# Linear attention, gated feed-forward and soft mixture on one core: where two kinds of early work stand in the VectorE and ScalarE queues

## The chip, the cores and the metric

One core of a Trainium2 chip. The metric is the device time of one execution in microseconds; the kernel as it was takes 327.0 us (median of 3 runs, 326.41 to 327.06).

## What is computed

Three layers on 4352 tokens (4 batches of 1088) of 128 features; every weight and activation is float32 at the interface.

```python
# attention with a feature map phi(x) = outer(S1 x, S2 x), 64 features per head
kv = einsum('bhsf,bhsd->bhfd', phi(k), v);  z = phi(k).sum(s)
x  = (phi(q) @ kv) / (phi(q) . z + 1e-6)
# gated feed-forward, d_ff = 1536
xn = x / sqrt(mean(x*x) + 1e-6) * rms_g
y  = (silu(xn @ w_gate) * (xn @ w_val)) @ w_out
# soft mixture of 8 experts with 4 slots each: softmax over tokens, expert MLP, softmax over slots
out = combine(y @ phi, experts(dispatch(y @ phi).T @ y))
```

S1, S2 and the three feed-forward weights arrive as 64-bit floats and are put together on the chip from their 32-bit words.

## The kernel before: tiles, stages and the order of the work

**Tiles and slots.** The tokens form nine tiles: tiles 0 to 7 hold 512 tokens each (two to a batch), tile 8 holds the 256 tokens left over. Within a tile the feed-forward goes over the 12 blocks of 128 of d_ff. One (tile, block) pair is a slot; slots are counted from 0 here, so slot 9 is the tenth and slots 0 to 11 are tile 0. In the main loop (`for i in range(n_slots + LAG)`) a slot does, on TensorE, a gate and a value product of three matmuls each (`mm3`, L621 to L623: high part by high part, high by low, low by high); on ScalarE the silu (L651); on VectorE the product of silu and value (L652, `ff_gate`), which reads the value's PSUM bank, of which there are two; and two slots later the product with w_out (`ff_out`). For tile 0, `ff_out` uses the whole w_out in two passes (L676, tile `ring`); only from tile 1, slot 12, does it use the split w_out, `woh` and `wol` (L621 to L623 with output `o`).

**Weights.** `w_keys` lists nine groups: gv0, o0, gv1, gv2, o1, gv3, gv4, o2, gv5. A gv group is 256 columns of w_gate and w_val and feeds two slots (gv1 slots 2 and 3, gv5 slots 10 and 11); an o group is a third of w_out. `f64_words` converts a group: two ScalarE passes (L189, L192), three VectorE passes (L194, L196, L198), an add on GpSimd (L202, in two pieces). `split_w` then makes the high part on ScalarE (L238, a cast) and the low part on GpSimd (L244, two pieces; for gv0 on VectorE, L246). For w_out, `split_o` calls `split_w` for the three groups in a row; it is put on the list of conversion steps at slot 9 (`if i == NF - 3`), so its three casts and six subtractions are written in the program after slot 9's `ff_gate`.

**Keys and queries.** `k_chain(b)` works for batch b (1 to 3; batch 0 is done ahead): two half groups g of VectorE transposes (`k.transpose`, L336, two instructions each, into tile `T`), a projection on TensorE (L354), feature products on VectorE (L282), sums on TensorE (L384), and at last the table `kvz` (L421). The odd 64 tokens of a batch go through TensorE (L339), a copy on ScalarE (L342, also into `T`) and L354. Batch 1's chain is spawned at slot 0 with a start at slot 8, so its transposes are written after the `ff_gate` of slot 9 (g = 0) and of slot 11 (g = 1); batch 2's after slots 25 and 27, batch 3's after slots 49 and 51. `q_chain(T)` prepares tile T's x: a transpose of the queries (`shuffle`, L492, also into `T`), a projection (L497), products, L520 against `kvz`, division, root (L566, L567 on GpSimd), scaling (L571), a TensorE transpose (L576), and the high and low parts xh (L581) and xl (L582). Tile `T` has two buffers for all of these.

**What sets the order.** After the first slot the code fixes no order of its own: a planner places each engine's instructions by its own estimate of when they are ready, and among ready ones takes the one written first. Each engine then runs its queue strictly in that order. `tc.issue_after(x)` puts what is traced inside it, as far as it runs on x's engine, behind x in that queue; it adds no wait for x to finish. `mark` holds such x: `mark["silu"]` the latest silu (ScalarE), `mark["gate", T, f]` the product of a slot (VectorE).

Of the kernel before, what the change touches and what calls it, by code (L numbers as in the profile page):

```python
# [12 lines left out]
ALU = mybir.AluOpType  # L13
# [35 lines left out]
def body(ctx, tc, q, k, v, s1, s2, wg, wv, wo, rg, phi, w1, w2, out):  # L49
    nc = tc.nc  # L50
    pe, act, dve, pool = nc.tensor, nc.scalar, nc.vector, nc.gpsimd
# [17 lines left out]
    def row(tag, bufs=1, dt=F32):  # L69
        return sb.tile([P, 512], dt, tag=tag, name=tag, bufs=bufs)  # L70
# [3 lines left out]
    gate = [None]  # L74
# [102 lines left out]
    mark = {}  # L177
# [38 lines left out]
    def conv_w(key):  # L216
        kind, i = key
        if kind == "gv":
            w = row("cvt", 2)
        else:  # L220
            if i % 2 == 0:
                wo_full[0] = ring()
            w = wo_full[0][:, 512 * (i % 2) : 512 * (i % 2) + 512]
            wo32.append(w)
        s, r = row("cvs", 2).bitcast(U32), row("cvc", 2).bitcast(U32)
        yield from f64_words(stage.pop(key), w, s, r, w.bitcast(U32))
        if kind == "gv":
            yield from split_w(key, w, dve if i == 0 else pool)

    def split_w(key, w, low):  # L230
        kind, i = key
        if kind == "gv":
            dh, dl = (t[:, :, 256 * i : 256 * (i + 1)] for t in (wgh, wgl))
            src = w.rearrange("p (m n) -> p m n", m=2)
        else:
            dh, dl = (t[:, 4 * i : 4 * i + 4, :] for t in (woh, wol))
            src = w.rearrange("p (c n) -> p c n", c=4)
        act.copy(dh, src)  # L238
        yield
        if low is pool:  # L240
            k = PIECE // src.shape[2]
            for t in range(0, src.shape[1], k):
                ts = slice(t, t + k)
                pool.tensor_tensor(out=dl[:, ts], in0=src[:, ts], in1=dh[:, ts].bitcast(F32), op=ALU.subtract)  # L244
        else:
            low.tensor_tensor(out=dl, in0=src, in1=dh.bitcast(F32), op=ALU.subtract)  # L246
        yield

    def split_o():

        for i, w in enumerate(wo32):
            yield from split_w(("o", i), w, pool)
# [188 lines left out]
    def k_chain(b):  # L441
        k = Keys(b)
        with tc.issue_after(mark["word"]):
            k.zero()
            for hp in range(2):
                k.copy_v(hp, pool.tensor_copy)
        for g in range(2):
            if g == 1:
                k.transpose(2)
            yield POST, 1  # L450
            k.transpose(g)
            if g == 1:
                k.copy(2)
            yield PE, 0
            k.project(g)
            yield POST, 1
            k.halves(g)
            k.outer(g)
            yield PE, 0
        k.project(2)  # L460
        yield POST, 1
        k.halves(2)
        k.outer(2)
        yield PE, 0
        for hp in range(2):
            k.sum(hp, range(9))
            yield PE, 1
        yield POST, 0
        k.spread()
        yield PE, 0  # L470
        k.back()
        yield POST, 1
        k.place()
        kv_done.add(b)
# [142 lines left out]
    hh, hl, hf32 = {}, {}, {}  # L617
# [15 lines left out]
    def pieces(T, f):  # L633

        return [slice(0, 256), slice(256, 512)] if (T, f) == (8, NF // 2 - 1) else [slice(0, 512)]
# [11 lines left out]
    def ff_gate(T, f):  # L647
        s = row("silu", 2)
        hf32[T, f] = row("hh", 3, F32R).bitcast(F32) if T == 0 and f < WHOLE else row("hf", 2)
        for g, v, cs in zip(gps.pop((T, f)), vps.pop((T, f)), pieces(T, f)):  # L650
            mark["silu"] = act.activation(s[:, cs], g[:, cs], AF.Silu).ins  # L651
            mark["gate", T, f] = dve.tensor_tensor(out=hf32[T, f][:, cs], in0=v[:, cs], in1=s[:, cs], op=ALU.mult).ins  # L652

    def whole(T, f):

# [246 lines left out]
    def start_tile(T):  # L902
# [9 lines left out]
        if T % 2 == 0 and T // 2 + 1 < B:  # L912
            b = T // 2 + 1
            load_k(b)
            load_q(b)
            load_kr(b)
            load_v(b)
            spawn(k_chain(b), PE, 8 if b == 1 else 0)
# [28 lines left out]
    for i in range(n_slots + LAG):  # L947
        now = base + i
        if i < n_slots:
            T, f = slots[i]  # L950
# [10 lines left out]
        if i < n_slots:  # L961
            in_order(ff_gate, T, f)
# [179 lines left out]
    for T in range(NTILE):  # L1142
# [10 lines left out]
        o = [ps.tile([P, 512], F32, tag="gv"[(T + e) % 2], name="fo", bufs=2) for e in range(2 if T == 0 else 1)]  # L1153
# [14 lines left out]
        if T < 8:  # L1168
            b, hf = T // 2, T % 2
            nc.sync.dma_start(  # L1170
                out=out[S * b : S * b + 1024].rearrange("(p j) d -> p j d", j=8)[:, 4 * hf : 4 * hf + 4, :], in_=ob
            )
        else:
            for hf in range(2):
                nc.sync.dma_start(
                    out=out.rearrange("(u e s) d -> e s u d", u=2, e=2)[hf, 1024:], in_=ob[64 * hf : 64 * hf + 64, 0:2, :]
# [31 lines left out]
```

## Time and profile before

| what | value |
|---|---|
| runs | 326.41, 327.06, 327.0 us (median 327.0) |
| the profiled execution: its own time | 326.61 us |
| its span in the profile | 324.8 us |
| TensorE busy | 312.0 us, 96% |
| VectorE / ScalarE / GpSimd busy | 237.5 / 185.4 / 61.2 us |
| granted TensorE clock, mean | 0.986 |

The span leaves 1.8 us of the execution's own time outside. Times in rows are microseconds from the start of the span. PE is TensorE, DVE VectorE, ACT ScalarE, POOL GpSimd, SP the engine that issues the loads. L12 is line 12 of the kernel. A number in brackets at the end of a timeline row is the engine's idle time just before it and what ended it. A granted clock of 1.00 is 2.4 GHz, 0.50 is 1.2 GHz.

### The profile page before, as it was taken

Reading aid. Unit: us, or ns where it says so; the run is one execution under the profiler, and the core shown is the slowest. Engines: PE = TensorE matmul, PEld = TensorE weight load, DVE = VectorE, ACT = ScalarE, POOL = GpSimd, SP = SyncE. Lnnn points to the kernel's source line nnn. Section 1 sums busy time; section 2 is a strip of 40 time slices with the busy share of each in tenths; the row PEclk is TensorE's granted clock in tenths of the full one; section 3 lists DMA queues with packets and bytes.
Section 4 is the critical chain, followed back from the end, with each engine's and each line's share of the span. In section 5 each row is a group of like instructions: output and inputs, shape, how many; then the busy total and the mean of one; then the engine's idle time right before and its main releaser. Section 6 shows DMA issues by size and latency. Waiting matters only on the chain.

```text
span 324.8 us, 5533 instructions
## 1 busy us (share of the span) xinstructions
PE 312.0 (96%) x2028; PEld 248.1 (76%) x2028; DVE 237.5 (73%) x458; ACT 185.4 (57%) x412; POOL 61.2 (19%) x104
## 2 busy tenths in 40 slices
PE   8987989999998999999999999999999999999994
PEld 6774655778886878888888778888888878897574
DVE  4779976775878785777887868678778666664663
ACT  3757464456565455665564657565656666556553
POOL 3356699700010210001001000010020100003030
PEclk9997899999999999999999999999999999999998
DMA  8988000000007000000070000000890394000007
GB/s 201 297 289 206 0 0 1 2 0 2 0 0 199 7 2 0 2 0 0 2 198 5 3 0 2 0 0 6 279 251 3 78 339 103 0 2 0 2 3 274
DMA packets 31131, 22.40 MB, mean 69 GB/s; under 512 B 13056, under 2 KB 27136, under 8 KB 31104
## 3 DMA queue, kind: packets, MB, share of 16 engines
q1 hardware_dynamic: 31072, 22.04, 23.6%
q8 instruction: 16, 0.26, 0.3%
q14 instruction: 11, 0.09, 0.1%
q10 hardware_dynamic: 32, 0.00, 0.0%
HBM read 19.81 MB, written 2.23 MB: 68 GB/s over the span
## 4 chain that ended last, share of the span: by engine, by line
PE 75%; issue 6%; DVE 5%; DMA 1%; POOL 1%; ACT 1%; DVEq 0%; SPq 0%; POOLq 0%
PE v L621 6%; PE g L621 6%; PE v L622 6%; PE g L622 6%; PE v L623 6%; PE g L623 6%; PE o L621 6%; PE o L622 6%; PE o L623 6%; PE aux L520 3%; PE aux L384 2%; PE aux L354 2%; PE aux L497 2%; PE o L676 2%; PE fo L1159 1%
## 5 line engine op out<-in xcount | busy, mean ns | idle before, releaser
L651 ACT ACTIVATE silu<-g 128x512 f32<-128x512 f32 (+1 forms) x103 | 60.5, 592 | 41.1 <-PE g L623 38.6
L661 ACT CAST hh<-hf 128x512 fp32r<-128x512 f32 x89 | 55.0, 617 | 42.3 <-DVE hf L652 38.8
L666 DVE TENSOR_TENSOR hl<-hf,hh 128x512 fp32r<-128x512 f32 x89 | 60.9, 685 | 22.4 <-ACT hh L661 21.0
L652 DVE TENSOR_TENSOR hf<-v,silu 128x512 f32<-128x512 f32 (+1 forms) x91 | 61.8, 680 | 19.7 <-PE v L623 9.5
L621 PE MATMUL v<-xh,wgh 128*128 128x512 f32 (+1 forms) x108 | 44.0, 408 | 2.1 <-DVE hh L652 1.6
L621 PE MATMUL g<-xh,wgh 128*128 128x512 f32 (+1 forms) x108 | 42.8, 402 | 1.0 <-ACT wgh L238 1.0
L622 PE MATMUL g<-xh,wgl 128*128 128x512 f32 (+1 forms) x108 | 42.7, 395 | 0.0
L622 PE MATMUL v<-xh,wgl 128*128 128x512 f32 (+1 forms) x108 | 42.1, 390 | 0.0
L623 PE MATMUL g<-xl,wgh 128*128 128x512 f32 (+1 forms) x108 | 41.4, 384 | 0.0
L623 PE MATMUL v<-xl,wgh 128*128 128x512 f32 (+1 forms) x108 | 41.0, 381 | 0.0
L621 PE MATMUL o<-hh,woh 128*128 128x512 f32 (+1 forms) x94 | 36.8, 392 | 0.0
L623 PE MATMUL o<-hl,woh 128*128 128x512 f32 (+1 forms) x94 | 36.6, 389 | 0.0
L622 PE MATMUL o<-hh,wol 128*128 128x512 f32 (+1 forms) x94 | 35.7, 380 | 0.0
L566 POOL TENSOR_SCALAR rs<-ss 128x4 f32<-128x4 f32 (+1 forms) x9 | 2.6, 290 | 138.8 <-ACT sq L561 137.2
L621 PEld LDWEIGHTS v<-xh,wgh 128*128 128x128 f32 x108 | 20.6, 190 | 8.7 <-DVE hh L652 3.8
L621 PEld LDWEIGHTS g<-xh,wgh 128*128 128x128 f32 x108 | 20.3, 191 | 5.8 <-ACT wgh L238 1.9
L622 PEld LDWEIGHTS g<-xh,wgl 128*128 128x128 f32 x108 | 20.6, 191 | 4.7 <-issue 0.8
L622 PEld LDWEIGHTS v<-xh,wgl 128*128 128x128 f32 x108 | 20.3, 188 | 4.7 <-issue 1.3
L623 PEld LDWEIGHTS g<-xl,wgh 128*128 128x128 f32 x108 | 20.6, 191 | 4.3 <-issue 0.5
L623 PEld LDWEIGHTS v<-xl,wgh 128*128 128x128 f32 x108 | 20.3, 188 | 4.6 <-issue 0.7
L621 PEld LDWEIGHTS o<-hh,woh 128*128 128x128 f32 x94 | 17.7, 188 | 3.0
L623 PEld LDWEIGHTS o<-hl,woh 128*128 128x128 f32 x94 | 17.7, 188 | 3.0
(254 smaller groups left out, 522.2 us busy)
## 6 DMA issues: line engine op xcount, KB each, us to landing
ring<-in_moe_w_dram SPq DMA_DIRECT2D x12, 256.0 KB, 6.5
ring<-in_moe_w_dram SPq DMA_DIRECT2D x5, 512.0 KB, 5.4
ring<-in_k_dram SPq DMA_DIRECT2D x8, 256.0 KB, 3.0
qt<-in_q_dram SPq DMA_DIRECT2D x4, 512.0 KB, 5.3
ring<-in_v_dram SPq DMA_DIRECT2D x16, 128.0 KB, 4.7
ring<-in_moe_w_gate_dram SPq DMA_DIRECT2D x6, 256.0 KB, 6.3
ring<-in_moe_w_val_dram SPq DMA_DIRECT2D x6, 256.0 KB, 6.5
ring<-in_moe_w_out_dram SPq DMA_DIRECT2D x3, 512.0 KB, 6.2
```

The lines of the kernel that those rows point to most:

```text
L354: pe.matmul(o, self.kT[g][:, P * t : P * t + pp], bdf, start=True, stop=True)
L384: pe.matmul(self.a["kv", hp][64 * h2 : 64 * h2 + D1, 64 * hp : 64 * hp + 64], va[:, h, 2 * i + g, :] if t < 8 else vr[:, h, :], self.pk[hp ...
L497: pe.matmul(self.a["q"][:, 64 * h : 64 * h + 64], self.qD[:, P * h : P * h + P], bdf, start=True, stop=True)
L520: pe.matmul(o, pD[:, f, h, :], rhs, start=(f == 0), stop=(f == 1))
L621: first = pe.matmul(o, ah, bh, start=start, stop=False)
L622: pe.matmul(o, al, bh, start=False, stop=False)
L623: last = pe.matmul(o, ah, bl, start=False, stop=stop)
L651: mark["silu"] = act.activation(s[:, cs], g[:, cs], AF.Silu).ins
L652: mark["gate", T, f] = dve.tensor_tensor(out=hf32[T, f][:, cs], in0=v[:, cs], in1=s[:, cs], op=ALU.mult).ins
L661: act.copy(hh[T, f], hf32[T, f])
L666: dve.tensor_tensor(out=hl[T, f], in0=hf32.pop((T, f)), in1=hh[T, f].bitcast(F32), op=ALU.subtract)
L676: last = pe.matmul(ops[T][:, 0:w], w_c, h[:, cs], start=(c == 0), stop=(c == NF - 1))
```

## The change

Three places, all of them order alone; no operand, size, engine or transfer is touched. The casts of w_out's split are queued behind the silu of the slot at which they are written (slot 9). Each pair of VectorE key transposes (g = 0 and 1, all three later batches) is queued behind the last product of silu and value written before it. `mark["gate"]` is new and holds that product.

```diff
@@ split_w
-        act.copy(dh, src)
+        with tc.issue_after(mark["silu"]) if kind == "o" else nullcontext():
+            act.copy(dh, src)
@@ k_chain
             yield POST, 1
-            k.transpose(g)
+            with tc.issue_after(mark["gate"]):
+                k.transpose(g)
@@ ff_gate
-            mark["gate", T, f] = dve.tensor_tensor(out=hf32[T, f][:, cs], in0=v[:, cs], in1=s[:, cs], op=ALU.mult).ins
+            mark["gate"] = mark["gate", T, f] = dve.tensor_tensor(out=hf32[T, f][:, cs], in0=v[:, cs], in1=s[:, cs], op=ALU.mult).ins
```

## Rows read from the trace of the kernel before

**Rows 1.** Page, part 1: busy us, share of the span and instructions

```profile
PE 312.0 (96%) x2028; PEld 248.1 (76%) x2028; DVE 237.5 (73%) x458; ACT 185.4 (57%) x412; POOL 61.2 (19%) x104
```

**Rows 2.** Stretches: length, busy us of each engine, PEclk, DMA share, GB/s

```profile
29.00:35.00 6.00, 5.47 (x10) 3.26 (x11) 5.97 (x12) 1.96 (x5) 2.26 (x4) 0.50 0.45 90
...
47.00:62.00 15.00, 14.35 (x63) 9.85 (x62) 9.13 (x11) 6.67 (x18) 14.27 (x24) 1.00 0.01 2
...
98.00:102.00 4.00, 3.13 (x17) 2.39 (x16) 2.76 (x5) 1.56 (x3) 0.00 (x0) 1.00 0.64 189
102.00:296.00 194.00, 194.00 (x1175) 160.64 (x1174) 145.54 (x268) 116.66 (x251) 12.63 (x20) 1.00 0.21 58
```

**Rows 3.** Waits of PE, whole span: waited for, total us, times, longest

```profile
PE v L621 <- DVE hh L652: 1.6, 3, 0.8
...
PE g L621 <- ACT wgh L238: 1.0, 2, 0.7
...
PE aux L354 <- DVE T L336: 0.9, 1, 0.9
...
PE aux L354 <- ACT T L342: 0.3, 1, 0.3
```

**Rows 4.** Timeline of PE, tile 0: start, us, instruction, [idle before <-releaser]

```profile
30.75 0.80 PE L621 MATMUL v<-xh,wgh 128*128 128x512 f32 x1 [0.52 <-DVE hh L652]
...
46.15 0.50 PE L621 MATMUL v<-xh,wgh 128*128 128x512 f32 x1 [0.77 <-DVE hh L652]
...
48.28 0.39 PE L621 MATMUL v<-xh,wgh 128*128 128x512 f32 x1
...
61.28 0.50 PE L622 MATMUL g<-xh,wgl 128*128 128x512 f32 x1
```

**Rows 5.** Timeline of DVE, tile 0

```profile
28.19 1.11 DVE L336 STREAM_TRANSPOSE T<-ring 128x256 f32<-128x256 f32 x2 [0.48 <-DMA ring<-in_k_dram]
29.15 0.82 DVE L194 TENSOR_SCALAR ring<-ring 128x512 f32<-128x512 f32 x1
30.00 0.69 DVE L652 TENSOR_TENSOR hh<-v,silu 128x512 f32<-128x512 f32 x1
...
31.47 0.41 DVE L194 TENSOR_SCALAR ring<-ring 128x512 f32<-128x512 f32 x1
...
32.40 1.08 DVE L336 STREAM_TRANSPOSE T<-ring 128x256 f32<-128x256 f32 x2
...
45.42 1.27 DVE L652 TENSOR_TENSOR hh<-v,silu 128x512 f32<-128x512 f32 x2
```

**Rows 6.** Timeline of POOL: w_out's low parts, and gv5's

```profile
28.26 1.42 POOL L244 TENSOR_TENSOR wol<-ring,woh 128x256 fp32r<-128x256 f32 x2
...
40.13 2.06 POOL L244 TENSOR_TENSOR wol<-ring,woh 128x256 fp32r<-128x256 f32 x2
...
56.44 1.86 POOL L244 TENSOR_TENSOR wol<-ring,woh 128x256 fp32r<-128x256 f32 x2
...
59.65 1.43 POOL L244 TENSOR_TENSOR wgl<-cvt,wgh 128x256 fp32r<-128x256 f32 x2
```

**Rows 7.** Timeline of ACT: the first of w_out's three casts

```profile
26.00 0.61 ACT L238 CAST woh<-ring 128x512 fp32r<-128x512 f32 x1
```

**Rows 8.** Timeline of DVE where tile 2 begins

```profile
100.66 1.09 DVE L336 STREAM_TRANSPOSE T<-ring 128x256 f32<-128x256 f32 x2 [1.20 <-DMA ring<-in_k_dram]
```

**Rows 9.** Timelines of PE, DVE and ACT: users of T, and of kvz

```profile
27.23 1.10 PE L497 MATMUL aux<-bd,T 128*128 128x64 f32 x8 [0.86 <-DVE T L492]
...
66.14 1.29 DVE L492 STREAM_TRANSPOSE T<-qt 128x512 f32<-128x512 f32 x2
...
94.71 1.00 PE L497 MATMUL aux<-bd,T 128*128 128x64 f32 x8
...
131.55 1.54 ACT L421 COPY kvz<-aux 32x264 f32<-32x264 f32 x4 [0.89 <-PE aux L412]
...
140.47 0.72 PE L520 MATMUL aux<-kvz,work 128*128 128x132 f32 x5
```

## The prediction

> **What bounds the kernel now.** I first read the page's busy shares: TensorE is busy 96% of the span [rows 1], so nothing but TensorE's own idle time, or time at the lower clock, can be won. Next the stretches: from 102 to 296 us it is busy without a gap [rows 2], so most of the kernel offers nothing. What is left lies in tile 0 (about 29 to 62 us) and where tile 2 begins (98 to 102 us, 0.87 us missing) [rows 2]. Then TensorE's list of waits: of the entries, those on work that the change touches or that stands near it are value matmuls waiting for VectorE's product of silu and value (1.6 us in 3 waits), gate matmuls waiting for ScalarE's cast of w_gate (1.0 us in 2), a key projection waiting for its transposes (0.9) and one waiting for the copy of the odd keys (0.3) [rows 3]. In the timeline of tile 0 the first group's waits are 0.52 us at 30.75 and 0.77 at 46.15 [rows 4]; the third is the remainder, about 0.3. So the question is what VectorE is doing when TensorE wants that product.
>
> In its queue, from 29 to 35 us VectorE is busy 5.97 of 6 us [rows 2]: there it, and not TensorE, sets the pace. And it holds key transposes of the second batch that the program writes only after slot 9's product: two at 28.19 (1.11 us, after 0.48 us of standing still for the key load) and two at 32.40 (1.08) [rows 5]. The first pair stands directly in front of what slot 0's product at 30.00 needs, and TensorE's value matmul at 30.75 waits for just that product [rows 4, 5]. On GpSimd w_out's low parts of groups o0 and o1 stand at 28.26 and 40.13, 1.42 and 2.06 us in the row of conversions [rows 6], though split weights of w_out are first read by slot 12, and slot 10 is still at its matmuls at 61.28 [rows 4].
>
> **Part 1, the transposes of batch 1.** Removed from VectorE's saturated stretch: 1.11 + 0.48 + 1.08 = 2.67 us [rows 5]. They go behind the products of slots 9 and 11, where VectorE is busy 9.13 of 15 us [rows 2], so their 2.2 us there I cost at nothing for VectorE; if that cover is gone, it costs at most these 2.2 us. Queued behind a pair there: the next product and tile 1's scaling; who waits are the batch's projections on TensorE.
>
> One thing comes in their place. Both T buffers are now free once tile 1's projection at 27.23 is done [rows 9]. Tile 3's query shuffle has no such tie, and in the trace it was taken as soon as a buffer was free: two shuffles stand at 66.14, but the projection of the second is at 94.71 [rows 9]. I expect it to move up into the early stretch, at 1.29 / 2 = 0.65 us. VectorE's net lead is then 2.67 - 0.65 = 2.0 us.
>
> **Part 2, w_out's split.** Three casts leave ScalarE's early queue. The first, at 26.00, is 0.61 us [rows 7] and stands directly before slot 0's silu; this costs nothing now, since VectorE is later still (30.00). Six subtractions leave GpSimd's row: 1.42 us ahead of gv1's low part and 2.06 us ahead of gv3's add [rows 6]. With VectorE's lead of 2.0 us, gv3's cast comes about 2 us earlier, against a wait for it of 0.3 us: 1.0 less the longest, 0.7 [rows 3], which is for gv1's cast, before anything that is moved but w_out's first cast, and which I leave. The third subtraction (1.86 us at 56.44) stands before gv5's low part at 59.65 [rows 6]. All six now come behind slot 9's silu, in 53 to 65 us. GpSimd is busy 14.27 of 15 us there [rows 2], but the only thing TensorE needs of it at once is gv5's low part; w_out's own is due at slot 12.
>
> *A rule against the rows.* VectorE's L194 took 0.82 us at 29.15, while GpSimd was at the first w_out piece, and 0.41 at 31.47 [rows 5, 6]. The Trainium skill, SBUF — State Buffer, section "Who interferes with whom", says that such a VectorE operation and a GpSimd one that reads SBUF exclude each other for a whole instruction through a shared port pair, and that one with a single SBUF input outside the fast modes doesn't. By this rule each w_out piece moved away would give VectorE up to 0.4 us besides, a lead near 3 us and no wait left in tile 0, and the sum below would be 0.2 us larger; but the next conversion moves up and collides in its stead, so I take the sum without it.
>
> **Part 3, batches 2 and 3.** Batch 2's first pair stood still 1.20 us for its load, at the head of VectorE's queue [rows 8], and TensorE's key projection then waited 0.9 us for it [rows 3]. Behind slot 25's product the load has landed, so this wait goes: between 0 and 0.87, I take 0.87. Batch 3's pair shows no wait of TensorE: nothing. No transfer is moved, and SP's queue stays; a load that is given its buffer later is not in sight, since loads wait for a tile's start.
>
> **The sum.** TensorE's idle time that goes: 0.52 at 30.75, which counts half since TensorE runs at half clock from 29 to 35 us (granted 0.50 [rows 2]) and I let that stretch stay where it is: 0.26. Then 0.77, 0.3 (cast), 0.3 (third product) and 0.87: together 2.5. Each matmul after a wait also takes 0.11 us longer (0.50 at 46.15 against 0.39 at 48.28 [rows 4]); for four, 0.45. That is 2.95 us. What comes new: batch 1's first projection now follows its transposes closely, and where a projection does, TensorE waited 0.86 (27.23 [rows 9]) or 0.9 [rows 3]; between 0 and 0.9 for each of two, in all I take 0.5. And the product at 46.15 comes later than it would need, since 0.5 + 0.3 of waits ahead of it go too and TensorE asks earlier: 0.8 + 0.8 against a lead of 2.0, close enough that I take 0.2 of a wait as left. So 2.95 - 0.5 - 0.2 = 2.25 us, say 2.3. The profiled execution took 326.61 us (span 324.8); it becomes 324.3. It was 0.4 us under the median of 327.0, so my forecast for the median is **324.7**, its own range 323.4 to 326.0.
>
> **Rivals.**
>
> *The conversions, not the transposes, hold tile 0 (smaller gain).* For it: gate casts wait for GpSimd's adds, and GpSimd is nearly full from 47 to 62 us [rows 2]. Against: the wait that I can read at 30.75 ends with VectorE. Then only batch 2's 0.87, the 0.26 and some 0.1 are won: 327.0 - 1.2 = 325.8.
>
> *w_out's pieces get in front of gv5's low part (no gain).* They now become ready at about the same time as gv5's cast. The third piece is before it already [rows 6]; the first two add 1.42 + 2.06 = 3.5 us, against a lead of 2 to 2.6, so that part ends near 62. TensorE meanwhile arrives about 2 us earlier than 61.28 [rows 4] and has no key projection left to fill the wait, so it idles near 3 us: the gain of tile 0 is gone and the 0.87 with it, 326.9. If the clock then falls as it did at 29 us, after such waits as the 0.86 at 27.23 [rows 9], half of 6 us comes on top [rows 2]: 330. The Trainium skill, TensorE: Matmul & The Clock Gate, section "HAM oscillation — how this bites in real kernels", has this rule, that waits of TensorE throttle its clock; by it the dearer of the two prices would be the right one whenever the wait is long. Against the rival: gv5's split is written earlier in the program and is taken first among ready work.
>
> *Slower: the two T buffers.* Batch 2's pairs now wait for slots 25 and 27, while tile 4's and tile 5's query shuffles are tied to nothing. If both take a T buffer before batch 2's second pair, that pair waits until a projection frees one, and a buffer was held so for 94.71 - 66.14 = 28.6 us [rows 9]. The batch's kvz is placed at 131.55 to 133.09 and first read at 140.47 [rows 9], a slack of 7.4 us. TensorE would then stall at tile 4 for anything from 0 to 21 us; I take 8: 327.0 - 2.3 + 8 = 332.7. It decides from the point where the pair comes more than 7.4 us later than now. Against it: the pair is written earlier than either shuffle, and both shuffles need the queries' load, which is issued behind the keys'.
>
> *The clock does not fall at 29 us.* Half of the 6 us at 0.50 [rows 2] is then won too, 3 us: near 322. Against: what TensorE does before 29 us is not touched.
>
> That the change doesn't do what it says I give no chance: the casts at 26.00 and the transposes at 28.19 and 32.40 stand in front of the instructions they are now tied behind.
>
> **How the numbers follow.** Forecast 0.58; conversions hold 0.16; no gain 0.10; the same with a lost clock 0.06; T buffers 0.06; clock stays 0.04. A measurement of this kernel tells about 0.2% (0.65 us) from no change, so faster means under 326.35. Faster: 0.58 + 0.16 + 0.04 = 0.78; same 0.10; slower 0.12. The range runs from 323.2 (the forecast's low end and a little) to 327.2, which takes in the case of no gain; outside stay the lost clock, the T buffers and the clock that stays, 0.16.
>
> **What would show it.** In the changed profile: no L336 on VectorE between 10 and 50 us; no w_out cast before slot 9's silu; slot 0's product done by about 29 us; TensorE's list with less than 0.6 us for value matmuls waiting for that product, no wait for a cast in tile 0 after 30 us, and no wait for batch 2's transposes at 100 us; gv5's low part before 60 us; the half-clock stretch still there and about 6 us long. I am wrong if TensorE idles at gv5's low part, if tile 0's waits only change their names, or if a gap opens at the start of tile 4.

## The result: 1% faster, a little more than forecast, and not where the forecast had put it

| | before | after |
|---|---|---|
| median of 4 runs | 326.84 us | 323.65 us |
| all runs | 326.41 to 327.06 | 323.34 to 324.17 |
| the profiled execution, its span | 326.61, 324.8 | 324.17, 322.3 |
| granted TensorE clock, mean | 0.986 | 0.991 |

The ratio is 0.9903, 95% interval 0.9887 to 0.9919: 3.2 us by the medians. The profiled executions are 2.44 us apart. Part of that difference lies ahead of everything that the change touches: the first matmul of the main loop (L621 before, L623 after, on xh) begins at 23.35 us in the trace of before and at 23.78 in that of after, and between 23.39 and 23.87 in the ten kernels below. Counted from that matmul, the copy of tile 3's output out of PSUM comes at 143.73 before and 140.72 after, 3.0 us earlier, and that is about what is left at the end. So I give the times inside tile 0 from that matmul on. Line numbers after the first place of the change have moved by one or two: L654 is the product of silu and value (before: L652), L337 a key transpose (L336), L245 a low part on GpSimd (L244), L355 the key projection (L354).

**Stretches after the change**, against [rows 2]. Columns as there: length, busy us of PE, PEld, DVE, ACT, POOL, granted clock, DMA share, GB/s.

```profile
29.00:35.00 6.00, 5.12 (x13) 3.27 (x13) 5.97 (x11) 3.00 (x7) 3.05 (x4) 0.72 0.56 124
...
47.00:62.00 15.00, 15.00 (x62) 10.41 (x61) 11.07 (x16) 7.11 (x16) 14.55 (x26) 1.00 0.01 2
...
98.00:102.00 4.00, 3.68 (x18) 2.97 (x18) 4.00 (x8) 2.52 (x6) 0.00 (x0) 1.00 1.11 287
102.00:293.00 191.00, 190.49 (x1158) 157.75 (x1158) 143.03 (x263) 114.69 (x247) 12.83 (x20) 1.00 0.20 55
```

VectorE is still without a pause from 29 to 35 us: what was taken out of its queue there was filled by the conversions behind it. The granted clock in that stretch is 0.72 where it was 0.50. From 47 to 62 us TensorE no longer pauses. From 62 to 293 us nothing was won: TensorE idles 0.32 us in 98 to 102 and 0.51 in the stretch behind, together 0.83, against 0.87 and none before [rows 2], and 0.27 us at 97.82 for a silu, where before it did not wait.

**TensorE's waits after**, against [rows 3]: waited for, total us, times, longest.

```profile
PE o L678 <- DVE hh L654: 1.1, 1, 1.1
...
PE aux L340 <- DMA kr<-in_k_dram: 0.8, 1, 0.8
...
PE v L623 <- DVE hh L654: 0.4, 1, 0.4
```

**Timeline of PE after**, against [rows 4].

```profile
29.88 2.05 PE L678 MATMUL o<-hh,ring 128*128 128x512 f32 x2 [1.11 <-DVE hh L654]
...
43.91 0.51 PE L623 MATMUL v<-xh,wgh 128*128 128x512 f32 x1 [0.41 <-DVE hh L654]
...
57.02 0.50 PE L624 MATMUL g<-xh,wgl 128*128 128x512 f32 x1
...
102.51 0.24 PE L340 MATMUL aux<-ident,kr 64*128 64x64 f32 x1 [0.83 <-DMA kr<-in_k_dram]
```

The waits for casts of w_gate are gone. The waits for the product of silu and value are not: 1.6 us in three became 0.4 in one, but the tile's w_out product, which stands first in line now, waits 1.11 us for slot 0's product at 29.88. And where tile 2 begins, the wait for batch 2's transposes [rows 3] has an heir of nearly the same length, the transpose of the odd keys on TensorE (L340), which waits 0.83 us for their load.

**Timeline of DVE after**, against [rows 5, 8]:

```profile
28.06 0.94 DVE L194 TENSOR_SCALAR ring<-ring 128x512 f32<-128x512 f32 x1
29.04 0.69 DVE L654 TENSOR_TENSOR hh<-v,silu 128x512 f32<-128x512 f32 x1
...
52.82 1.09 DVE L337 STREAM_TRANSPOSE T<-ring 128x256 f32<-128x256 f32 x2
...
59.97 1.11 DVE L337 STREAM_TRANSPOSE T<-ring 128x256 f32<-128x256 f32 x2
...
99.00 1.11 DVE L337 STREAM_TRANSPOSE T<-ring 128x256 f32<-128x256 f32 x2
```

**Timelines of POOL and ACT after**, against [rows 6, 7]:

```profile
29.45 1.62 POOL L245 TENSOR_TENSOR wgl<-cvt,wgh 128x256 fp32r<-128x256 f32 x2 [0.73 <-ACT wgh L239]
...
54.88 1.43 POOL L245 TENSOR_TENSOR wgl<-cvt,wgh 128x256 fp32r<-128x256 f32 x2
56.25 4.26 POOL L245 TENSOR_TENSOR wol<-ring,woh 128x256 fp32r<-128x256 f32 x6
...
51.57 1.65 ACT L239 CAST woh<-ring 128x512 fp32r<-128x512 f32 x3
```

The order is the one that the change asks for. Batch 1's transposes stand behind products of tile 0, without any wait of their own, and the projections that follow them on TensorE, at 55.88 and 64.09, show no wait either. The six pieces of w_out's low part come in one row at 56.25, directly behind gv5's low part at 54.88: gv5's part ends at 56.3, and TensorE asks for it at 57.02. That is a margin of 0.7 us, of which more below.

### The profile page after: what moved, and what is told of

The parts are those of the page before. It is cut to its first block, busy times and chain, and to the rows that moved or that the text cites. A ratio compares the mean times of both kernels' runs of the same rounds, so it can differ in the third digit from the quotient of the medians.

```text
span 322.3 us, 5538 instructions
## 1 busy us (share of the span) xinstructions
PE 310.7 (96%) x2028; PEld 247.8 (77%) x2028; DVE 237.0 (74%) x458; ACT 185.0 (57%) x412; POOL 61.3 (19%) x104
## 4 chain that ended last, share of the span: by engine, by line
PE 78%; issue 5%; DVE 2%; DMA 1%; SPq 1%; POOL 0%; ACT 0%; DVEq 0%; POOLq 0%
PE v L623 7%; PE g L624 6%; PE v L624 6%; PE g L625 6%; PE v L625 6%; PE g L623 6%; PE o L623 6%; PE o L625 6%; PE o L624 6%; PE aux L522 4%; PE o L678 3%; PE aux L385 2%; PE aux L355 2%; PE aux L499 2%; DMA kr<-in_k_dram 1%
## 5 line engine op out<-in xcount | busy, mean ns | idle before, releaser
L654 DVE TENSOR_TENSOR hf<-v,silu 128x512 f32<-128x512 f32 (+1 forms) x91 | 61.3, 679 | 20.4 <-PE v L625 11.4
L623 PE MATMUL v<-xh,wgh 128*128 128x512 f32 (+1 forms) x108 | 44.1, 408 | 0.8 <-DVE hh L654 0.4
L623 PE MATMUL g<-xh,wgh 128*128 128x512 f32 (+1 forms) x108 | 43.4, 406 | 0.3 <-ACT silu L653 0.3
L624 PE MATMUL g<-xh,wgl 128*128 128x512 f32 (+1 forms) x108 | 42.0, 389 | 0.0
L623 PE MATMUL o<-hh,woh 128*128 128x512 f32 (+1 forms) x94 | 36.8, 392 | 0.0
L568 POOL TENSOR_SCALAR rs<-ss 128x4 f32<-128x4 f32 (+1 forms) x9 | 3.0, 333 | 132.4 <-ACT sq L563 130.8
L623 PEld LDWEIGHTS v<-xh,wgh 128*128 128x128 f32 x108 | 20.5, 190 | 6.6 <-DVE hh L654 1.2
L623 PEld LDWEIGHTS g<-xh,wgh 128*128 128x128 f32 x108 | 20.6, 191 | 5.7 <-ACT silu L653 1.0
L624 PEld LDWEIGHTS o<-hh,wol 128*128 128x128 f32 x94 | 17.7, 188 | 2.9
```

Of the source, the lines that this page charges most:

```text
L623: first = pe.matmul(o, ah, bh, start=start, stop=False)
L624: pe.matmul(o, al, bh, start=False, stop=False)
L654: mark["gate"] = mark["gate", T, f] = dve.tensor_tensor(out=hf32[T, f][:, cs], in0=v[:, cs], in1=s[:, cs], op=ALU.mult).ins
```

## The experiments

Each experiment is compared with runs of the kernel before that were taken together with it: 326.98 us (median of 23) for e1 to e4, 326.98 (of 17) for e5 to e8, 326.95 (of 15) for e9 and e10. All diffs are against the changed kernel.

### The change taken apart: four kernels

**Keys alone.** The cast's tie is taken out again.

```diff
@@ e1_keys_only, split_w
-        with tc.issue_after(mark["silu"]) if kind == "o" else nullcontext():
-            act.copy(dh, src)
+        act.copy(dh, src)
```

> The key transposes of batches 1 to 3 are tied as in the change, w_out's casts are free as before. Theory A (VectorE's queue held tile 0; w_out's split matters little): 324.0 us, at least 2.5 us faster than before, the value matmuls' waits for the product under 0.8 us, the half-clock stretch after 29 us clearly shorter than 6.4 us. Rival B (GpSimd's and ScalarE's row of conversions held tile 0, so w_out's split is the half that pays): 326 us, and the casts of w_gate still wait.

**w_out alone.** The transposes' tie is taken out again.

```diff
@@ e2_wout_only, k_chain
-            with tc.issue_after(mark["gate"]):
-                k.transpose(g)
+            k.transpose(g)
```

> w_out's casts are tied as in the change, the key transposes are free as before. Theory A: 326.3 us, no more than 0.8 us faster than before; the transposes still stand in VectorE's queue around 28 and 32 us and the value matmul behind slot 0's product still waits; half-clock stretch about 6.4 us. Rival B: 324.3 us.

**Batch 1's keys alone, and those of batches 2 and 3 alone** (the cast's tie is out in both):

```diff
@@ e3_keys_b1 (e4_keys_b23: b > 1), k_chain
-            with tc.issue_after(mark["gate"]):
+            with tc.issue_after(mark["gate"]) if b == 1 else nullcontext():
```

> Only batch 1's key transposes are tied; batches 2 and 3 and w_out's casts are as before. Theory A (batch 1 alone pays, and at tile 2 the wait for the transposes only changes its name to one for the odd keys' load): within 0.4 us of the kernel with all three batches tied, about 324.0 us, with the 0.87 us wait of the projection at tile 2 back. Rival, the forecast's part 3 (batch 2's tie is worth 0.87 us): 0.9 us slower than the kernel with all three tied.

> Only the key transposes of batches 2 and 3 are tied; batch 1's and w_out's casts are as before. Theory A: 326.8 us, within 0.5 us of before, TensorE idle at the start of tile 2 as long as before (0.9 us) or longer but behind the odd keys' load. Rival, the forecast's part 3: 325.9 us.

Measured, with the time from the first matmul of the main loop to the end of the product of slots 0, 4 and 10 (from the rows of L652 or L654 in each trace):

| kernel | median us (runs) | ratio, 95% | slot 0 | slot 4 | slot 10 |
|---|---|---|---|---|---|
| before | 326.98 (23) | | 7.34 | 22.75 | 40.38 |
| batches 2, 3 alone (e4) | 326.41 (11) | 0.9988, 0.9973 to 1.0002 | 6.66 | 22.62 | 40.27 |
| batch 1 alone (e3) | 325.03 (12) | 0.9953, 0.9939 to 0.9966 | 5.96 | 21.03 | 37.06 |
| all keys (e1) | 324.73 (5) | 0.994, 0.9928 to 0.9952 | 5.95 | 21.02 | 37.05 |
| the whole change | 323.65 (4) | 0.9903, 0.9887 to 0.9919 | 5.95 | 20.08 | 35.68 |
| w_out alone (e2) | 330.36 (6) | 1.0094, 1.0062 to 1.0125 | 6.37 | 22.03 | 35.12 |

So batch 1's transposes are worth 326.98 - 325.03 = 1.95 us, those of the later batches another 325.03 - 324.73 = 0.3, and w_out's split on top of both another 324.73 - 323.65 = 1.1. And w_out's split without the keys *costs* 3.4 us, which no theory had foreseen. The 0.3 is not clear of noise: the runs of e3 spread from 324.77 to 326.86 us, and the later batches alone (e4) cannot be told from nothing. The profiled execution of e3 is its slowest, with a granted clock of 0.83 from 300 to 310 us, so its trace is used for tile 0 only.

Against the expectations: e1 gained 2.25 us and not the 2.5 of its theory A, but is nearer to it than to rival B. e3 is within the 0.4 us of e1 that its theory A allowed. e4 lies between its two theories, and TensorE's wait for the odd keys at tile 2 is only 0.20 us there. e2 refutes both of its own.

**What w_out's split brings beside the keys** stands on GpSimd. Timeline of POOL with the keys alone (e1):

```profile
28.68 1.60 POOL L244 TENSOR_TENSOR wol<-ring,woh 128x256 fp32r<-128x256 f32 x2
30.23 1.79 POOL L244 TENSOR_TENSOR wgl<-cvt,wgh 128x256 fp32r<-128x256 f32 x2
```

Here gv1's low part is done at 32.0 us, behind a piece of w_out; with the whole change it is done at 31.1 (row at 29.45 above), and both kernels start their main loop at 23.78. What waits for it is the next group's first conversion pass on ScalarE (L189), since the low part is the last to read the buffer `cvt`. That pass in e1, timeline of ACT:

```profile
32.06 0.69 ACT L189 ACTIVATE cvt<-ring 128x512 f32<-128x512 f32 x1 [1.97 <-POOL wgl L244]
```

and in the changed kernel:

```profile
31.11 0.68 ACT L189 ACTIVATE cvt<-ring 128x512 f32<-128x512 f32 x1 [1.01 <-POOL wgl L245]
```

It comes 0.95 us earlier, slot 4's product 0.94, slot 10's 1.37.

**What it costs without the keys** stands on GpSimd too, 20 us later. Timelines of POOL and PE, and stretches, with w_out alone (e2):

```profile
55.40 1.42 POOL L245 TENSOR_TENSOR wgl<-cvt,wgh 128x256 fp32r<-128x256 f32 x2
56.78 4.17 POOL L245 TENSOR_TENSOR wol<-ring,woh 128x256 fp32r<-128x256 f32 x6
...
61.12 1.03 POOL L568 TENSOR_TENSOR rs<-rs,mhalf 128x4 f32<-128x4 f32 x1
...
34.00:37.00 3.00, 0.23 (x1) 0.00 (x0) 3.00 (x6) 0.00 (x0) 1.83 (x2) 1.00 0.00 0
...
37.21 1.13 PE L677 MATMUL o<-hh,ring 128*128 128x512 f32 x2 [2.98 <-DVE hh L653]
...
63.06 1.09 PE L577 MATMUL aux<-ident,x 128*128 128x128 f32 x4 [2.38 <-DVE x L572]
...
40.00:60.00 20.00, 19.18 (x76) 12.55 (x75) 11.88 (x22) 11.31 (x26) 18.41 (x27) 1.00 0.00 0
60.00:63.00 3.00, 0.69 (x2) 0.00 (x0) 0.74 (x1) 0.59 (x1) 2.90 (x6) 1.00 0.00 0
63.00:70.00 7.00, 6.94 (x25) 5.96 (x25) 2.19 (x3) 1.17 (x3) 1.35 (x7) 0.51 0.01 2
```

The six pieces, 4.17 us, stand in front of tile 1's root (L568 at 61.12). VectorE's scaling waits for the root, TensorE's transpose of x waits for the scaling and has almost nothing else to do from 60 to 63 us, and the 7 us behind that run at 1.2 GHz. With the keys tied too, the root came at 52.97, ahead of all pieces.

### Two tests of w_out's place on GpSimd

If that reading holds, the loss must vanish when nothing but GpSimd's order is mended; and what w_out's split gains must not need the casts on ScalarE.

```diff
@@ e9_wout_root: as w_out alone, and besides
@@ split_w (low part on GpSimd)
-                pool.tensor_tensor(out=dl[:, ts], in0=src[:, ts], in1=dh[:, ts].bitcast(F32), op=ALU.subtract)
+                with tc.issue_after(mark["root"]) if kind == "o" else nullcontext():
+                    pool.tensor_tensor(out=dl[:, ts], in0=src[:, ts], in1=dh[:, ts].bitcast(F32), op=ALU.subtract)
@@ q_chain
-            pool.tensor_tensor(out=self.rs, in0=self.rs, in1=mhalf[:, 0:n], op=ALU.pow)
+            mark["root"] = pool.tensor_tensor(out=self.rs, in0=self.rs, in1=mhalf[:, 0:n], op=ALU.pow).ins
```

> w_out's casts tied as in the change, the key transposes not; besides, w_out's six subtractions on GpSimd are queued behind tile 1's root. Theory A (alone, w_out's split loses because its six pieces, 4.17 us, stand in front of tile 1's root, so that TensorE waited 2.38 us for the scaled x and then ran at half clock for some 7 us): both go, the list of TensorE's waits has no entry for x above 1 us, and about 4 to 5 of 330.4 us go: 325.9, within 325.2 to 326.8, the key transposes still early. Rival F (it loses on ScalarE or in VectorE's early queue, whatever GpSimd's order): still 329 or more.

Measured: 325.03 us (5 runs, 324.75 to 325.35), ratio 0.9932, interval 0.991 to 0.9955. Slots 0 and 4 end their products where w_out alone ends them (6.36 and 22.01). POOL in this kernel:

```profile
57.21 1.03 POOL L569 TENSOR_TENSOR rs<-rs,mhalf 128x4 f32<-128x4 f32 x1
58.21 4.62 POOL L246 TENSOR_TENSOR wol<-ring,woh 128x256 fp32r<-128x256 f32 x6
```

The root stands 3.9 us earlier, no wait for x is left but the 0.9 us that every kernel has at the start, and 5.3 us are back. Theory A holds, with a time a little under its range (325.2 to 326.8), and rival F is out: w_out's split alone, with its pieces behind the root, is a gain of 1.9 us, and the order of seven instructions on GpSimd turned it into a loss of 3.4.

The second kernel keeps the keys' tie and the tie of the pieces behind the root, and frees the casts:

```diff
@@ e10_pieces_only: the two places of e9_wout_root, the keys tied, and
@@ split_w
-        with tc.issue_after(mark["silu"]) if kind == "o" else nullcontext():
-            act.copy(dh, src)
+        act.copy(dh, src)
```

> The key transposes tied as in the change; of w_out's split only the six subtractions on GpSimd are tied, behind tile 1's root, where the change has them too; the three casts on ScalarE are free and go early again. Theory A (what w_out's part adds beside the keys comes from GpSimd: without the early pieces its adds for the converted weights, and so the casts of w_gate and w_val, come earlier): 323.7 as with the whole change, product of slot 4 about 20.1 us after the first matmul of the main loop. Rival F (it comes from ScalarE, where the early casts stand in front of silus): 324.7 as with the keys alone, product of slot 4 at about 21.0 us.

Measured: 328.6 us (11 runs, 327.64 to 330.04), ratio 1.0049, interval 1.0033 to 1.0066. Both theories missed the time; on what they were to tell apart A holds: slot 4's product ends at 19.91 us, as early as with the whole change, though one cast of w_out stands directly before slot 0's silu again. Up to slot 4 an early cast on ScalarE costs nothing, and an early piece on GpSimd does. POOL and PE of this kernel, and two stretches, show where the rest went:

```profile
52.91 4.60 POOL L245 TENSOR_TENSOR wol<-ring,woh 128x256 fp32r<-128x256 f32 x6
...
58.86 1.41 POOL L245 TENSOR_TENSOR wgl<-cvt,wgh 128x256 fp32r<-128x256 f32 x2
...
59.62 0.50 PE L624 MATMUL g<-xh,wgl 128*128 128x512 f32 x1 [3.06 <-POOL wgl L245]
...
58.00:62.00 4.00, 2.38 (x7) 1.92 (x8) 0.16 (x1) 1.30 (x3) 3.68 (x10) 0.78 0.00 0
62.00:64.00 2.00, 2.00 (x7) 1.58 (x6) 1.83 (x4) 0.00 (x0) 0.57 (x3) 0.58 0.03 8
```

The pieces were ready as soon as the root was done, and went ahead of gv5's low part. TensorE waits 3.06 us for that, then runs partly at the lower clock. So in the changed kernel the casts' place behind slot 9's silu does matter, for a reason that is not ScalarE's: there gv5's cast ran first (at 50.55, w_out's at 51.57), and gv5's low part went ahead of the pieces. In e10 the last of w_out's casts ran at 46.48 and gv5's at 49.97. The tie alone does not ensure the order: e8, below, has it too, but there w_out's casts ran first (at 51.90, gv5's at 53.45), and the pieces went first.

### The lower clock at 29 us: is it a price?

The forecast let that stretch stand and counted a wait in it half. The kernel with the keys of batches 2 and 3 alone answers by chance: its VectorE queue holds batch 1's transposes early, at 28.16 and 32.76, much as before [rows 5], and yet the profiled execution was granted the full clock earlier. Stretches and TensorE's waits of e4:

```profile
31.00:34.00 3.00, 3.00 (x6) 1.67 (x5) 3.00 (x6) 0.79 (x2) 0.95 (x2) 0.50 0.36 75
34.00:36.00 2.00, 2.00 (x8) 1.27 (x7) 2.00 (x5) 1.09 (x2) 0.62 (x1) 0.97 0.00 0
...
PE g L622 <- ACT wgh L238: 2.2, 3, 1.2
PE v L622 <- DVE hh L653: 1.4, 3, 0.8
```

Before, the granted clock was 0.50 from 29 to 35 us [rows 2]; here it is 0.97 from 34 us. The time that TensorE saved so came back as waiting: for casts of w_gate 2.2 us instead of 1.0 [rows 3], and slot 4's product ends at 22.62 instead of 22.75.

Two kernels from above make a closer pair. In e2 and e9 VectorE runs the same instructions in the same order from the first matmul to slot 4's product. The granted clock in e2 is 1.00 from 26 to 60 us; in e9 it is 0.72 from 29 to 35 us. One stretch of e2, then a stretch and a wait of e9:

```profile
31.00:34.00 3.00, 3.00 (x12) 1.88 (x10) 3.00 (x7) 1.63 (x3) 0.00 (x0) 1.00 0.25 42
...
29.00:35.00 6.00, 5.60 (x15) 3.56 (x16) 5.97 (x13) 2.85 (x6) 1.62 (x2) 0.72 0.54 109
...
PE o L678 <- DVE hh L654: 1.9, 2, 1.5
```

Slot 4's product ends at 22.03 in e2 and 22.01 in e9. The longest wait for slot 2's product is 2.98 us in e2 (at 37.21) and 1.5 in e9: what TensorE gained by the full clock, it waited. A kernel that fills TensorE's pause with idle matmuls tests it on purpose:

```diff
@@ e6_busy: keep_busy(10) behind tile 1's projection, the first w_out product behind it
+        if T == 1:
+            with tc.issue_after(mark["project"]):
+                keep_busy(10)
...
+                with tc.issue_after(mark["busy"]):
+                    last = pe.matmul(ops[T][:, 0:w], w_c, h[:, cs], start=(c == 0), stop=(c == NF - 1))
```

> The changed kernel, and besides 10 matmuls on constant data (no result used) stand on TensorE between the queries' projection of tile 1 and the first product with w_out, where TensorE idles 1.11 us and its clock then falls. Theory A (tile 0 runs at VectorE's pace, TensorE's lower clock is hidden): the half-clock stretch gets shorter or goes, and the time is 323.6 us within 0.4, with longer waits of TensorE in its place. Rival D (the half-clock stretch after 29 us is what the change shortened, and costs half its length): 322.0 us.

Measured: 324.11 us (4 runs, 323.98 to 324.33), ratio 0.9915, interval 0.9902 to 0.9927. The granted clock is 1.00 up to 310 us, and the time is no better than the changed kernel's: 0.1 us above what theory A allowed, and 2.1 above rival D. TensorE's waits of e6:

```profile
PE g L626 <- ACT wgh L239: 1.1, 1, 1.1
...
PE v L626 <- DVE hh L657: 0.8, 1, 0.8
PE aux L522 <- DVE work L510: 0.7, 1, 0.7
```

The changed kernel waits 0, 0.4 and 0.2 us in these places, and its slot 4's product ends at 20.08 where that of e6 ends at 20.33. What TensorE gains by the clock it stands still for afterwards: the converted weights and the products set the pace there.

This holds for that stretch of tile 0 and not everywhere. The runs of e3 with a mean clock of 0.997 or 0.998 took 324.77 to 325.14 us, those with 0.986 took 326.86, and the trace of one of these shows a second fall of the clock at 300 to 310 us. There a lower clock goes with a longer time.

### What is ahead of slot 0's product, and the next candidates

Two conversion passes (0.61 and 0.94 us) still stand in front of slot 0's product at 29.04. This kernel moves both behind it:

```diff
@@ e5_words_late, f64_words: for gv2 and o1
-        dve.tensor_scalar(out=t, in0=t, scalar1=2.0, scalar2=None, op0=ALU.max)
+        with tc.issue_after(mark["gate", 0, 0]) if late else nullcontext():
+            dve.tensor_scalar(out=t, in0=t, scalar1=2.0, scalar2=None, op0=ALU.max)
```

> The changed kernel, and besides the first VectorE pass of conversion groups gv2 and o1 is queued behind slot 0's product (in the changed kernel both stand in front of it, 0.61 and 0.94 us, and TensorE waits 1.11 us for that product). Theory A (VectorE's order sets the pace of tile 0; what stands in front of the product TensorE waits for costs its time): the 1.11 us wait shrinks to 0.2 and the kernel takes 322.8 us, 0.8 us less than the changed one. Rival C (VectorE's total work sets the pace up to slot 8 or so, not its order): the wait moves to a later product and the time stays at 323.6 us.

Measured: 324.32 us (6 runs, 323.49 to 324.98), ratio 0.9921, interval 0.9907 to 0.9935: not faster than the changed kernel, and nearer to rival C than to theory A. DVE and PE of e5:

```profile
27.58 0.69 DVE L655 TENSOR_TENSOR hh<-v,silu 128x512 f32<-128x512 f32 x1
...
28.69 0.75 DVE L195 TENSOR_SCALAR ring<-ring 128x512 f32<-128x512 f32 x2
...
36.06 3.55 PE L523 MATMUL aux<-kvz,work 128*128 128x132 f32 x16 [2.78 <-DVE work L511]
```

Slot 0's product comes 1.4 us earlier (4.55 us after the first matmul) and the 1.11 us wait is gone; at 36.06 TensorE waits 2.78 us instead, and slot 4's product ends at 20.9, later than the 20.08 of the changed kernel. An early wait of TensorE was traded for a later and longer one.

**The odd keys.** Their transpose on TensorE is queued behind the last product of three matmuls, or tile 0's product with w_out, that is written before it:

```diff
@@ e7_odd_late, k_chain
-                k.transpose(2)
+                with tc.issue_after(mark["mm3"]):
+                    k.transpose(2)
```

> The changed kernel, and besides the odd keys' transpose on TensorE is queued behind the last product with w_out written before it. Theory A (at tile 2 the wait for the transposes was only replaced by one of 0.83 us for the odd keys' load): that wait falls under 0.3 us and the kernel takes 323.0 us, 0.7 less than the changed one. Rival: something else is late there by as much, 323.6 us.

Measured: **322.76 us** (4 runs, 322.59 to 323.44), ratio 0.9876 to before, interval 0.9864 to 0.9889, 0.9 us under the changed kernel. Tile 0 is as there (slots 0, 4, 10 at 5.95, 20.05, 35.66). Timeline of PE at tile 2 of e7:

```profile
100.73 0.55 PE L355 MATMUL aux<-bd,T 128*128 128x64 f32 x4
101.87 0.55 PE L355 MATMUL aux<-bd,T 128*128 128x64 f32 x4
102.65 0.27 PE L340 MATMUL aux<-ident,kr 64*128 64x64 f32 x1
```

Both projections run first and the odd keys have landed by then: no wait is left in this stretch. Theory A holds, and this kernel is the fastest of all.

**Tile 1's queries later** (its chain started at slot 3, tied behind the last product):

```diff
@@ e8_q_late
-        with tc.issue_after(mark["gate", 1, 0] if T == 2 else mark["sq0"]) if T < 3 else nullcontext():
+        with tc.issue_after(mark["gate"] if T == 1 else mark["gate", 1, 0]) if T < 3 else nullcontext():
...
-            spawn(q_chain(T + 1), POST)
+            spawn(q_chain(T + 1), POST, 3 if T == 0 else 0)
```

> The changed kernel, and besides tile 1's query chain starts at slot 3, its transpose behind that slot's product: some 3 us of VectorE work leave the stretch from 27 to 38 us. Theory A (VectorE's total work there is the pace): 322.5 us, 1.1 us less than the changed kernel, if tile 1's xh is still ready at slot 12. Rival E (xh of tile 1 becomes the late one): slower than 324 us, with a wait of TensorE behind tile 1's scaling.

Measured: 326.2 us (12 runs, 325.7 to 327.89), ratio 0.9983, interval 0.9971 to 0.9994. Rival E has the time and the wait right. POOL of e8 (its profiled execution took 327.32 us):

```profile
54.70 4.16 POOL L245 TENSOR_TENSOR wol<-ring,woh 128x256 fp32r<-128x256 f32 x6
58.81 1.42 POOL L245 TENSOR_TENSOR wgl<-cvt,wgh 128x256 fp32r<-128x256 f32 x2
```

Slot 4's product ends at 19.36, earlier than in any other kernel, and it is lost again where tile 0 ends: the pieces went ahead of gv5's low part (TensorE waits 1.29 us for it) and ahead of the root (60.80), and TensorE waits another 1.05 us for x at 62.75. How much of the wait for x is the late start of the chain, and how much the pieces ahead of the root, was not separated.

## Why the prediction was right in size and direction, and wrong in its parts

The forecast of 324.7 us was 1.05 us too high; the sign and the range held. The sum of 2.25 us divides, by its own terms, into about 1.27 for batch 1 (0.26 + 0.77 + 0.3 + 0.3 and three restarts of 0.11, less 0.5 and 0.2), 0.98 for the later batches (0.87 and one restart) and nothing for w_out. Measured: 1.95, 0.3 and 1.1. Too little for batch 1 and too much for the later batches, 0.68 us each, cancel; that is luck, and the miss of the whole is w_out's.

**Batch 1: right in kind, and the step that failed is adding up TensorE's waits with the half-clock stretch held fixed ("I let that stretch stay where it is").** By the waits alone the forecast looks good: it had 1.2 us of them going in the net, and the six bracketed waits of tile 0 from 29 to 62 us came to 0.67 + 0.52 + 0.35 + 0.77 + 0.35 + 0.30 = 2.96 us before, and 1.11 + 0.16 + 0.41 = 1.68 are there after. But they are not the same waits: the 0.67 us for gv1's cast, which the forecast left, went, and 1.11 us for slot 0's product came, which it did not have. And the granted clock from 29 to 35 us rose from 0.50 to 0.72, 1.3 us of full-clock time, which was left out. The two were treated as separate purses. The runs show that they are one: with the clock up earlier (e4) the time went into waits for casts, with the same order on VectorE and another clock (e2, e9) slot 4 came at the same time, and with the clock at 1.00 (e6) nothing was won. TensorE isn't what sets the pace from 29 to 47 us, so the sum of its waits is not a measure of what can be won there. The page gave the better measure: 2.67 us of VectorE's time were taken out of a stretch in which VectorE is busy 5.97 of 6 us. That is an upper bound: slot 4's product then came 1.72 us earlier (e3), near the 1.95 of the end.

**The hoisted shuffle: did not come.** I took 0.65 us off VectorE's lead for tile 3's query shuffle. In the changed trace the two shuffles behind tile 1's stand here (timeline of DVE):

```profile
64.94 0.71 DVE L494 STREAM_TRANSPOSE T<-qt 128x512 f32<-128x512 f32 x1 [0.88 <-PE aux L355]
...
66.14 0.70 DVE L494 STREAM_TRANSPOSE T<-qt 128x512 f32<-128x512 f32 x1
```

No instruction wrote T between tile 1's shuffle at 26.90 and batch 1's transposes at 52.82, and yet the first of these two waits 0.88 us for a projection of batch 1 to release a buffer: it reads as buffers handed out in the order in which the program writes their users. The slower rival, two shuffles that overtake a key transpose, rested on the same freedom and did not come either. Nor was the price for projections behind late transposes (0.5 us) paid.

**The later batches: the wait went, and the next one stood behind it.** The term of 0.87 was taken at its full size because "the load has landed". It had, for the transposes (99.00, no wait). But before, TensorE came to the odd keys' transpose (105.03) only after both projections and found the keys there; after, it came right behind the first projection (102.51) and 0.83 us ahead of them. How long this new wait is varies with the kernel: 0.71 us in e1, 0.20 in e4, none in e5. I had asked, for every added wait, who is queued behind it, and had not asked what stands behind a wait that is removed. Moving that transpose (e7) made up 0.9 us, so the term had about the right size and was only not free to be taken by this change.

**w_out: the step that failed is costing six subtractions on GpSimd at no more than a cast's wait of 0.3 us.** I read that the 1.42 and 2.06 us pieces stand in the row of conversions and then looked only for the TensorE wait that they end. The first pair delays gv1's low part, that the next conversion's first pass, and the rest follows: 1.1 us at the end (e1 against the whole change), by GpSimd's order and not by ScalarE's (e10). I followed the row to TensorE and skipped the buffer that it holds.

**The rivals.** "The conversions hold tile 0" was given 0.16 as an alternative; it is half of the truth, since VectorE's transposes and GpSimd's pieces delay the same chain. "w_out's pieces get in front of gv5's low part" did not happen in the change, where gv5's part ended 0.7 us before TensorE asked for it, but it happened in two experiments: a wait "near 3 us" was forecast, e10 waited 3.06 and e8 1.29. The ground given against this rival, that gv5's split is written earlier and so taken first, held in the change and failed in these two. The Trainium skill, TensorE: Matmul & The Clock Gate, section "HAM oscillation — how this bites in real kernels", says that pauses of TensorE throttle its clock; e10 agrees (0.78 and 0.58 in the stretches behind the wait), and e2 shows a pause of 2.98 us after which the clock stayed. With its lost clock e10 takes 328.6, between the two prices given, 326.9 and 330. One rival was missing: that the pieces block tile 1's root (e2), which is the same crowd on GpSimd, one customer further.

**What was to show it.** Right: no key transpose on VectorE before 50 us, no cast of w_out before slot 9's silu, no cast wait, no wait for batch 2's transposes, gv5's low part before 60 us. Right by the letter only: value matmuls wait under 0.6 us for the product, but the w_out product waits 1.11 for it. Wrong: slot 0's product ends at 29.7 us and not by 29. Of this, 0.43 us is the later start of the main loop in that trace; and the two conversion passes that stood ahead of it before (0.61 us at 27.10, 0.82 at 29.15) are still there, at 0.61 and 0.94. Wrong too: the stretch at the lower clock is not 6 us long (0.72 in 29 to 35 us, against 0.50).

## What to carry to other kernels

Where an engine off the matmul path is busy without a pause, count what leaves *its* queue and follow the one product that TensorE asks for; the waits and the clock of TensorE in such a stretch are two forms of the same slack: a price for either alone is no price. When work is moved late, look where it lands and which short, urgent instruction stands behind it there: taking the same six subtractions out of GpSimd's early queue was worth -1.9 us where they landed behind tile 1's root and +3.4 in front of it (e9, e2, keys early), and, with the keys late, -1.1 behind gv5's low part and +3.9 in front of it (the whole change and e10, against e1). And for each wait that you take away, name what the waiting engine does next and when its input lands: that is where 0.83 of 0.87 us went here.

## What the runs showed that was not expected

A pause of TensorE and the granted clock behind it do not go by the wait's length alone. In e2 a wait of 2.98 us at 37.21 was followed by a clock of 1.00 (40 to 60 us), and the shorter one of 2.38 us at 63.06 by 0.51 for 7 us; ahead of the first TensorE was busy 0.23 of 3 us (34 to 37 us), ahead of the second 0.69 of 3. And the same order of work on VectorE in tile 0 went with 0.72 from 29 to 35 us in one profile (e9) and with 1.00 in another (e2). Why is not shown.

The same kind of VectorE pass (L194, in e5 L195) takes 0.94 us at 28.06 in the changed kernel, with GpSimd at an add until 28.7, and two of them together 0.75 us at 28.69 in e5, where GpSimd pauses from 28.5 to 29.2. The Trainium skill, SBUF — State Buffer, section "Who interferes with whom", gives a shared port pair as the reason; the trace agrees in direction, and no run here shows the port itself. The prediction was right that nothing is won by this in the change: the next conversion moved up and met GpSimd in the transposes' stead.
